# Sixteen words of padding behind a shared SBUF area, in a fused kernel of sliding-window attention and a ReLU MLP

## The chip, the cores and the metric

The kernel runs on one core of one Trainium2 chip. The metric is the device time of one execution in microseconds, taken as the median of several runs. Engines are named as the profile names them: PE (TensorE, matmuls), PEld (its weight loads), DVE (VectorE), ACT (ScalarE), POOL (GpSimd), SP (SyncE, which issues most DMAs).

## The reference

A layer over 2048 positions of width 576 adds an attention branch and an MLP branch, both on the normalized input, to the input:

```
xn  = layernorm(x)                               # x: (1, 2048, 576)
q, k, v = split(xn @ wqkv)                       # 32 heads of 18, wqkv: (576, 1728)
logits[s, w] = q[s] . k[s - 2 w] * 18 ** -0.5    # w = 0..7, masked where s - 2 w < 0
A = (softmax over w of logits, times v[s - 2 w]) @ wo      # wo: (576, 576)
B = relu(xn @ w1) @ w2                           # w1: (576, 4608), w2: (4608, 576)
out = x + A + B
```

Everything is float32 at the ends.

## The kernel before

**Phases.** The positions are dealt to two phases (even and odd), each with 1024 positions in four blocks of 256 (`NTB`, `TBN`). Within a phase the MLP's 36 hidden blocks of 128 run in two manners: six of them plainly (slots of `h_two` and `o_two`), the other thirty in 15 pairs by a seven-product scheme of Strassen's kind (`prologue`, `group`, `tail_end`). A group has eight steps; each step runs one list of products of input and W1 (`rows(...)`), and then half a piece of the second product, hidden block by W2 (`o_half`). QKV products (`qkv_half`, by four units of eight heads), attention on DVE (`attention`, fed piece by piece by `run_bg`), and the WO products (`wo_block`) are put in between. The whole order is written out by hand and by a planner that counts a matmul time of its own; the tile framework adds the waits.

**Precision.** Each float32 operand is split into a high and a low part in float32r (`two`: ACT copies the high part, DVE or POOL subtracts), and a product is a sum of three products: high by high, high by low, low by high.

**Matmuls.** Most matmuls use half of the array's rows: `mm_rows` and `rows` issue them alternately on the lower and the upper 64 partitions, so they come in pairs. In `nc.tensor.matmul(o, l, r)`, `l` is the weights operand (128 columns) and `r` is the moving operand. In the profile they stand under two lines, L140 (`mm_rows`) and L161 (`rows`); full-height ones at the start stand under L128. By tile names:

- `ph`/`pm <- xT,ar` and `xS,ar`: input (or its Strassen sums in xS) moving, 256 columns; weights are W1 or its sums, kept in `ar`.
- `po <- ar`: W2 moving, in two column parts of 256 and 320 (`CUT`); weights are the hidden blocks. Both are kept in `ar`.
- `po`/`pm <- wq,xT`: wqkv moving, 432 columns, kept in `wq` from word 60 on, with a pitch of 448 words (`WQ0`, `WQS`); weights are the input in `xT`.
- `po <- wq,att`, `wq,xS`, `att` and `att,xS`: WO moving, in parts of 256 and 320; weights are the transposed attention output.

**SBUF.** Tiles lie in a partition one after the other, in the order in which the pools are opened. In words of 4 bytes: small constants, xT (4 buffers of 2560), xS (2 of 4096 each), att (one of 68 x 144 = 9792), ar (11200), st2 (2 of 576), wq, ST (2048), and then buffers for products, evictions and small statistics. Inside `ar`: W1 and its sums from 0 on (multiples of 128 words), W2's 256-column part from 5168 (3 slots of 512), its 320-column part from 6720 (3 slots of 640), hidden blocks from 8640 (5 slots of 512):

```
W1_AT, W2A_AT, W2B_AT, H_AT, AR_WORDS = 0, 5168, 6720, 8640, 11200
```

**The area att.** The one buffer of `atp` is used by turns: for x, for q, k, v and the logits of attention (`att`), and, when attention is over, as `ot_arena`: the transposed attention output stands in 12 slots of 640 words (`ot_home`; four further slots are in xS), and behind them, from word 12 x 640 = 7680 on, stand three of the ten WO matrices of 576 columns each (`wo_rest`). The other seven stand in `wq` from its word 0 on (`wo_first`). Each WO matrix is used by `wo_half` as the moving operand, in the column parts of `CUT`.

Of the kernel before, what the change touches and what calls it, by code (L numbers as in the profile page):

```python
# [11 lines left out]
F32 = mybir.dt.float32  # L12
F32R = mybir.dt.float32r
# [6 lines left out]
P = 128  # L20
# [24 lines left out]
    (5, 0, 'xt', 6),  # L45
    (6, 0, 'xt', 7),
)
ROWS, Q_ROW, LG_ROW, K_ROW, V_ROW = 68, (15, 0), 8, 23, (38, 53)
X_AT = (2160, 2736, 0, 576, 7632, 8208, 5472, 1152)
HALO = ((0, 112), (112, 127))  # L50
# [18 lines left out]
def tile_body(ctx: ExitStack, tc: tile.TileContext, x, wqkv, wo, w1, w2, out):  # L69
    nc = tc.nc  # L70
    S, D = x.shape
    F = w1.shape[1]
    Dh = 18
    UD = HG * Dh
# [17 lines left out]
    atp = pool("atp", 1)  # L92
# [84 lines left out]
    W1, WQ, WO = {}, {}, {}  # L177
# [38 lines left out]
    def wq_load(ph, u):  # L216
        if ph == 0 and u == 0:
            z = prp.tile([P, 5, 3 * UD], F32, name="pr")
        else:
            k = V_ROW[1 if u == 0 else u % 2] * UD  # L220
            z = att(ph)[:, k : k + 15 * UD].rearrange("p (k c) -> p k c", k=5)
        WQR[ph, u] = z
        c = slice(u * UD, (u + 1) * UD)
        for kt in range(KT + 1):
            v = z[:, kt, :].rearrange("p (s c) -> p s c", s=3)
            if kt < KT:
                nc.sync.dma_start(v, wq_src[kt * P : (kt + 1) * P, :, c])
            else:
                for part in LOW, UPP:
                    nc.sync.dma_start(v[part], wq_src[KT * P : D, :, c])  # L230
# [13 lines left out]

    def wo_rest(ph):
        z = ot_arena(ph)
        WO[ph] += [z[:, 12 * 640 + k * D : 12 * 640 + (k + 1) * D] for k in range(3)]
        for kt in range(2, KT + 1):
            wo_load(ph, kt)

    def wo_load(ph, kt):
        lo = f32(WO[ph][5 + kt])
        if kt < KT:
            nc.sync.dma_start(lo, wo2[kt * P : (kt + 1) * P, :])
        else:
            for part in LOW, UPP:
                nc.sync.dma_start(lo[part], wo2[KT * P : D, :])
# [7 lines left out]
    hold = {}  # L265

    ATT = {}

    def att(ph):
        if ph not in ATT:  # L270
            ATT[ph] = atp.tile([P, ROWS * UD], F32, name="att")
        return ATT[ph]

    def ot_arena(ph):
        if ("ota", ph) not in hold:
            hold["ota", ph] = atp.tile([P, ROWS * UD], F32R, name="att")
        return hold["ota", ph]

    def load_x(i):
        z = att(0)  # L280
        k = X_AT[i]
        X[0, i] = z[:, k : k + D]
        if i < 2:
            for h, q in enumerate((nc.sync, nc.scalar)):
                c = slice(h * D2, (h + 1) * D2)
                q.dma_start(X[0, i][:, c], x_v[0, i][:, c])
            return
        nc.sync.dma_start(X[0, i], x_v[0, i])
# [28 lines left out]
    def norm(ph, i, act=False):  # L317
        nm, r = MR.pop((ph, i))
        if "xn" not in hold:
            hold["xn"] = att(0)[:, K_ROW * UD : K_ROW * UD + 1920].rearrange("p (k c) -> p k c", k=3)  # L320
        xn = hold["xn"][:, xn_count[0] % 3, 0:D]
        xn_count[0] += 1
        if act:
            nc.scalar.activation(xn, X[ph, i], AF.Identity, bias=nm)
            nc.scalar.activation(xn, xn, AF.Copy, scale=r)
        else:
            nc.vector.tensor_scalar(xn, X[ph, i], nm, r, op0=ALU.subtract, op1=ALU.mult)
            dve(600)
        XN[ph, i] = xn
# [306 lines left out]
    def ot_home(ph, i, k):  # L636
        n = 4 * WOB[ph].index(i // 2) + 2 * (i % 2) + k
        if n < 12:
            return ot_arena(ph)[:, 640 * n : 640 * (n + 1)]
        if ("otx", ph) not in hold:  # L640
            hold["otx", ph] = xsp.tile([P, 4, 640], F32R, name="xS")
        return hold["otx", ph][:, n - 12, :]
# [427 lines left out]
    def ot_plan(ph):  # L1070
        z = OTQ[ph] = []
        attended = lambda: all((ph, i) in ready for i in range(NI))
        free = lambda: attended() and ("xs", ph) in hold
        z.append(("wl", wo_rest, (ph,), attended, ()))
        for kt in range(2, KT + 1):
            z.append((("ws", kt), wo_split, (ph, kt), None, (("wl", 8 + 1.4 * (kt - 2)),)))
        for r in range(NTB):
            for i in (2 * WOB[ph][r], 2 * WOB[ph][r] + 1):
                before = 2 * WOB[ph][r - 1] + i % 2 if r else None
                z.append((("load", i), ot_load, (ph, i), attended, ((("turn", before), 0.0),) if r else ()))  # L1080
                z.append((("turn", i), ot_turn, (ph, i), None, ((("load", i), 6.0),) + (((("out", before), 4.0),) if r else ())))
                z.append((("out", i), blocks_out, (ph, i), None, ((("turn", i), 1.2),)))
                z.append((("in", i), ot_in, (ph, i), attended if r < 3 else free, ((("out", i), 5.0),)))
                z.append((("split", i), ot_split, (ph, i), None, ((("in", i), 7.0),)))
# [458 lines left out]
```

## Time and profile before

| | us |
|---|---|
| median of 3 runs | 1226.68 |
| lowest, highest of them | 1225.77, 1229.62 |
| the profiled execution, its own time | 1222.26 |
| its span, first to last instruction | 1220.5 |
| PE busy in the span | 1146.2 |
| PEld busy | 1123.8 |
| DVE busy | 813.7 |
| ACT busy | 574.9 |
| POOL busy | 473.1 |

The mean granted clock of PE in the profiled execution was 0.98. Busy times are of the span; PE and PEld overlap. A row of a group of instructions gives the line, the engine, the operation, output and inputs by tile names, the shape, the count, the busy time in us, the mean time of one in ns, and the idle time of the engine before them with what ended it. A matmul's time there holds its streaming and a fixed latency, and the latencies of consecutive matmuls overlap. A row of the timeline or of the chain gives the start in us, the length in us and what ran, with a count where equal instructions are drawn together.

### The profile page before, as it was taken

How to read it: one execution, taken by the hardware profiler on the slowest of the kernel's cores; microseconds unless marked ns; L12 is line 12 of the kernel's file. 1: busy time of each engine (PE TensorE's matmuls, PEld its weight loads, DVE VectorE, ACT ScalarE, POOL GpSimd, SP SyncE). 2: the span in 40 equal slices, each digit the busy share in tenths (PEclk: the TensorE clock that was granted, in tenths of full speed). 3: DMA queues.
4: the chain of work that ended last, by engine and by line, in shares of the span. 5: the costliest groups of instructions: out<-in, count | busy, mean ns of one | idle time of the engine just before them, and what ended most of it. 6: DMA issues, size and time to landing. Idle time of an engine off the chain costs nothing.

```text
span 1220.5 us, 38506 instructions
## 1 busy us (share of the span) xinstructions
PE 1146.2 (94%) x16410; PEld 1123.8 (92%) x16410; DVE 813.7 (67%) x1241; ACT 574.9 (47%) x1332; POOL 473.1 (39%) x522
## 2 busy tenths in 40 slices
PE   8997799999999999993899999999999999999797
PEld 8997799999999999993799999999999999999696
DVE  7564689598698687952422628876986886878331
ACT  4444564364454455552442435644644544555441
POOL 2214453353344345541221234524624533555221
PEclk9999899999999999998999999999999999999999
DMA  6467696697696588899976537857956967888996
GB/s 206 144 164 159 135 185 116 137 179 126 133 180 123 127 171 140 157 204 214 207 141 98 108 66 158 150 119 142 187 115 131 192 113 157 146 149 150 218 199 158
DMA packets 207131, 186.23 MB, mean 153 GB/s; under 512 B 69984, under 2 KB 152672, under 8 KB 206928
## 3 DMA queue, kind: packets, MB, share of 16 engines
q0 software_dynamic: 39744, 81.41, 44.9%
q1 hardware_dynamic: 166352, 101.48, 29.9%
q8 instruction: 129, 2.11, 0.7%
q10 hardware_dynamic: 864, 0.89, 0.2%
q14 instruction: 42, 0.34, 0.1%
HBM read 78.79 MB, written 100.42 MB: 147 GB/s over the span
## 4 chain that ended last, share of the span: by engine, by line
PE 72%; DMA 10%; SPq 5%; DVE 5%; issue 4%; ACT 4%; POOL 1%; ACTq 0%; DVEq 0%; POOLq 0%
PE po L161 22%; PE po L140 17%; PE ph L161 12%; PE pm L161 9%; PE pm L140 5%; PE ph L140 3%; DMA out<-ev 2%; SPq L387 2%; DMA words<-pr 2%; DVE ar L174 2%; ACT ev L703 1%; DMA att<-in_x 1%; SPq L397 1%; PE ph L128 1%; DMA xT<-words 1%
## 5 line engine op out<-in xcount | busy, mean ns | idle before, releaser
L161 PE MATMUL po<-ar 64*128 64x320 f32 (+1 forms) x5760 | 474.8, 293 | 1.5 <-DVE ar L174 0.7
L161 PEld LDWEIGHTS po<-ar 64*128 64x128 f32 x5760 | 418.1, 187 | 5.0 <-DVE ar L174 3.3
L708 POOL DMA_DIRECT2D out<-ev x276 | 244.0, 1023 | 457.1 <-ACT ev L703 429.1
L161 PE MATMUL ph<-xT,ar 64*128 64x256 f32 x2520 | 332.6, 281 | 11.7 <-ACT ar L170 6.2
L161 PEld LDWEIGHTS ph<-xT,ar 64*128 64x128 f32 x2520 | 293.7, 187 | 16.6 <-ACT pm L958 8.1
L161 PE MATMUL pm<-xS,ar 64*128 64x256 f32 x2160 | 270.4, 282 | 21.6 <-ACT u L962 15.4
L703 ACT ACTIVATE ev<-po 128x512 f32<-128x512 f32 (+1 forms) x276 | 177.7, 649 | 231.3 <-PE po L161 124.6
L161 PEld LDWEIGHTS pm<-xS,ar 64*128 64x128 f32 x2160 | 242.9, 188 | 24.1 <-ACT u L962 15.6
L174 DVE TENSOR_TENSOR ar<-st,ar 128x512 fp32r<-128x512 f32 (+3 forms) x232 | 150.4, 660 | 52.1 <-ACT ar L170 49.7
L172 POOL TENSOR_TENSOR ar<-st,ar 128x256 fp32r<-128x256 f32 (+1 forms) x72 | 94.1, 1310 | 182.5 <-ACT ar L170 180.3
L170 ACT ACTIVATE ar<-st 128x256 fp32r<-128x256 f32 (+3 forms) x304 | 148.1, 500 | 32.8 <-DMA st<-in_w 27.4
L890 POOL TENSOR_TENSOR st<-st 128x256 f32<-128x256 f32 x120 | 137.4, 1157 | 16.0 <-DMA st<-in_w 11.6
L140 PE MATMUL po<-wq,xT 64*128 64x432 f32 x1296 | 136.2, 355 | 0.0
L140 PEld LDWEIGHTS po<-wq,xT 64*128 64x128 f32 x1296 | 121.5, 184 | 3.3
L161 PE MATMUL ph<-xS,ar 64*128 64x256 f32 x720 | 107.5, 283 | 10.5 <-ACT ph L958 10.3
L161 PEld LDWEIGHTS ph<-xS,ar 64*128 64x128 f32 x720 | 97.5, 189 | 12.4 <-ACT ph L958 11.7
L560 DVE TENSOR_TENSOR pr<-att 128x1152 f32<-128x1152 f32 x64 | 87.8, 1377 | 11.3 <-DMA att<-att 11.1
L595 DVE TENSOR_TENSOR pr<-att 128x1152 f32<-128x1152 f32 x64 | 88.3, 1399 | 0.3
L563 DVE TENSOR_REDUCE att<-pr 128x64 f32<-128x1152 f32 x64 | 84.9, 1339 | 0.0
L140 PE MATMUL po<-ar 64*128 64x256 f32 (+1 forms) x984 | 75.0, 297 | 10.3 <-ACT ev L703 10.3
L140 PEld LDWEIGHTS po<-ar 64*128 64x128 f32 x984 | 68.8, 188 | 12.1 <-ACT ev L703 11.9
L602 DVE TENSOR_TENSOR pr<-pr 128x1152 f32<-128x1152 f32 x64 | 73.0, 1141 | 1.4
(117 smaller groups left out, 1313.7 us busy)
## 6 DMA issues: line engine op xcount, KB each, us to landing
out<-ev POOLq DMA_DIRECT2D x276, 288.0 KB, 5.8
st<-in_w SPq DMA_DIRECT2D x72, 288.0 KB, 4.6
st<-in_w SPq DMA_DIRECT2D x120, 128.0 KB, 4.1
att<-att SPq DMA_DIRECT2D x16, 441.0 KB, 4.5
att<-in_wqkv SPq DMA_DIRECT2D x28, 216.0 KB, 5.9
od<-att SPq DMA_DIRECT2D x32, 144.0 KB, 3.1
pr<-od SPq DMA_DIRECT2D x16, 288.0 KB, 4.9
words<-pr SPq DMA_DIRECT2D x64, 72.0 KB, 4.1
```

The costliest lines, as they stand in the source:

```text
L140: ins = nc.tensor.matmul(o, l[z], r[z], start=start, stop=stop)
L161: b.ins = nc.tensor.matmul(b.ap, l[part], r[part], start=start, stop=stop, skip_group_check=skip)
L170: nc.scalar.activation(hi, src, AF.Copy)
L172: nc.gpsimd.tensor_tensor(lo, src, f32(hi), op=ALU.subtract)
L174: nc.vector.tensor_tensor(lo, src, f32(hi), op=ALU.subtract)
L560: nc.vector.tensor_tensor(pr[i], q, window(k, i), op=ALU.mult)
L563: nc.vector.tensor_reduce(lg[:, i], pr.pop(i).rearrange(heads, d=Dh), axis=AX.X, op=ALU.add)
L595: nc.vector.tensor_tensor(pr[i].rearrange(heads, d=Dh), e, window(v, i).rearrange(heads, d=Dh), op=ALU.mult)
L602: nc.vector.tensor_tensor(o, z[:, :, 0:n], z[:, :, n : 2 * n], op=ALU.add)
L703: nc.scalar.activation(acc[:, :, cols], z[:, :, 0 : cols.stop - cols.start], AF.Copy)
L708: nc.gpsimd.dma_start(o_v[ph, 2 * tb + k], acc[:, k, :], accum_op=ALU.add)
L890: nc.gpsimd.tensor_tensor(stg(o), stg(a), stg(b), op=op)
```

## The change

The buffer of att gets 16 words more, so every tile allocated behind it (ar, st2, wq, ST and all later ones) moves up by 16 words, 64 bytes, in every partition; xT, xS and att itself stay where they are. The three WO matrices in att move up by the same 16 words within it. The view of att that attention uses keeps its size. No instruction that computes or moves data is added, removed or put elsewhere in its queue. In the built program PE, POOL and SP have the same waits as before; ACT has 14 more, each ahead of a copy of QKV results into att (L520 in `qkv_half`), for DVE's work on att in `attention`, and DVE has 6 more, each ahead of a product with v (L595 in `av_mul`), for such a copy.

```diff
+PAD = 16
 ROWS, Q_ROW, LG_ROW, K_ROW, V_ROW = 68, (15, 0), 8, 23, (38, 53)
...
     def wo_rest(ph):
         z = ot_arena(ph)
-        WO[ph] += [z[:, 12 * 640 + k * D : 12 * 640 + (k + 1) * D] for k in range(3)]
+        WO[ph] += [z[:, 12 * 640 + PAD + k * D : 12 * 640 + PAD + (k + 1) * D] for k in range(3)]
...
     def att(ph):
         if ph not in ATT:
-            ATT[ph] = atp.tile([P, ROWS * UD], F32, name="att")
+            ATT[ph] = atp.tile([P, ROWS * UD + PAD], F32, name="att")[:, 0 : ROWS * UD]
         return ATT[ph]
 
     def ot_arena(ph):
         if ("ota", ph) not in hold:
-            hold["ota", ph] = atp.tile([P, ROWS * UD], F32R, name="att")
+            hold["ota", ph] = atp.tile([P, ROWS * UD + PAD], F32R, name="att")
         return hold["ota", ph]
```

## The prediction

> **What bounds the kernel now.** I read the page first (busy shares, chain), then the stretches, then who waits for whom.
>
> ```profile
> span 1220.5 us, 38506 instructions
> PE 1146.2 (94%) x16410; PEld 1123.8 (92%) x16410; DVE 813.7 (67%) x1241; ACT 574.9 (47%) x1332; POOL 473.1 (39%) x522
> ...
> PE 72%; DMA 10%; SPq 5%; DVE 5%; issue 4%; ACT 4%; POOL 1%; ACTq 0%; DVEq 0%; POOLq 0%
> ```
>
> ```profile
> 200.00:500.00 300.00, 297.08 (x4370) 292.37 (x4369) 237.37 (x323) 150.44 (x361) 133.00 (x142) 1.00 0.75 145
> ```
>
> The columns are the stretch, its length, and the busy time of PE, PEld, DVE, ACT and POOL, then the granted clock. In this stretch PE is busy for 297.1 of 300 us, 99%, at clock 1.00, while DVE stands at 79%; the second phase has the like of it. The rest is the start, the seam between the two phases and the tail, where transfers and SP's queue enter the chain. So there is little waiting to remove: in the long stretches the time is the number of matmuls times the time of one, and a change of layout can act only on the latter.
>
> Matmuls run in pairs, one on the lower and one on the upper 64 rows, so a group of x instructions is x/2 pairs. This is what they are (mean ns of one, which is the streaming time and a latency of about 160 ns together):
>
> ```profile
> L161 PE MATMUL ph<-xT,ar 64*128 64x256 f32 x2520 | 332.6, 281 | 11.7 <-ACT ar L170 6.2 <-ACT pm L958 4.7 <-DVE ar L741 0.7
> L161 PE MATMUL pm<-xS,ar 64*128 64x256 f32 x2160 | 270.4, 282 | 21.6 <-ACT u L962 15.4 <-DVE u L967 5.5
> L161 PE MATMUL po<-ar 64*128 64x320 f32 x2880 | 261.4, 309 | 1.5 <-DVE ar L174 0.7
> L161 PE MATMUL po<-ar 64*128 64x256 f32 x2880 | 215.6, 278 | 0.0
> L140 PE MATMUL po<-wq,xT 64*128 64x432 f32 x1296 | 136.2, 355 | 0.0
> L161 PE MATMUL ph<-xS,ar 64*128 64x256 f32 x720 | 107.5, 283 | 10.5 <-ACT ph L958 10.3
> L161 PE MATMUL pm<-xT,ar 64*128 64x256 f32 x360 | 65.6, 287 | 0.1
> L140 PE MATMUL ph<-xT,ar 64*128 64x256 f32 x702 | 48.5, 286 | 3.2 <-ACT ar L170 2.3 <-DVE ar L174 0.9
> L140 PE MATMUL pm<-wq,xT 64*128 64x432 f32 x432 | 45.4, 355 | 0.0
> L140 PE MATMUL po<-ar 64*128 64x256 f32 x492 | 44.4, 283 | 8.9 <-ACT ev L703 8.9
> L140 PE MATMUL po<-wq,att 64*128 64x320 f32 x264 | 23.4, 306 | 0.0
> L140 PE MATMUL po<-wq,att 64*128 64x256 f32 x264 | 19.8, 280 | 0.0
> ```
>
> Between PE's 256-column groups lie several ns per matmul although the instruction is the same. That difference is the subject here. The time per pair comes from starts in the timeline (start, length, what):
>
> ```profile
> 621.88 1.36 PE L140 MATMUL po<-wq,att 64*128 64x256 f32 x20
> 623.08 0.40 PE L140 MATMUL po<-att 64*128 64x256 f32 x4
> ...
> 623.56 1.63 PE L140 MATMUL po<-wq,att 64*128 64x320 f32 x20
> 625.03 0.46 PE L140 MATMUL po<-att 64*128 64x320 f32 x4
> ...
> 301.40 0.88 PE L161 MATMUL ph<-xT,ar 64*128 64x256 f32 x12
> 302.12 0.86 PE L161 MATMUL po<-ar 64*128 64x256 f32 x12
> ...
> 241.97 0.86 PE L161 MATMUL po<-ar 64*128 64x256 f32 x12
> 242.67 0.87 PE L161 MATMUL ph<-xT,ar 64*128 64x256 f32 x12
> 243.37 0.86 PE L161 MATMUL po<-ar 64*128 64x256 f32 x12
> ```
>
> Ten WO pairs of 256 columns take 623.08-621.88, 120 ns each; ten of 320 take 147 ns each. So 64 more columns cost 27 ns, 0.42 ns a column. Six pairs on xT take 0.72 us in one place and 0.70 in another: 120 and 117 ns a pair. Six pairs of W2's 256-column half take 0.70 us, 117 ns, and they get faster inside the run: the group mean of a late slice of that same run (242.40 to 242.62) is 273, against 278 for the whole group:
>
> ```profile
> L161 PE MATMUL po<-ar 64*128 64x256 f32 x8 | 0.6, 273 | 0.0
> ```
>
> A WO matmul at 120 ns a pair lasts 280 ns (its group above), so 273 means 113 ns a pair: W2's half settles at 113, while WO settles at 120.
>
> **What the change does to the positions.** Count each operand's first word modulo 64 words, from the start of xT. Tiles stand in the order in which their pools are opened, and xT (4 x 2560 words), xS (2 x 4096), att (9792), ar (11200), st2 (2 x 576) are all multiples of 64, so each starts at 0. A pair streams its moving operand while the weights of the next pair are read. I call "lead" the weights' position less the moving operand's.
> - xT or xS moving at 0, weights in ar at 0: lead 0. After, ar starts at 16: lead 16.
> - W2's 256-column half, at 5168 in ar, which is 48; weights (the hidden slots at 8640) at 0: lead 16. After, both move: lead 16.
> - W2's 320-column half, at 6720, which is 0: lead 0 before and after.
> - QKV, at 60 in wq, over xT at 0: lead 4. After, 76, which is 12: lead -12.
> - WO at 0 in wq and att, over the transposed attention output at 0: lead 0. After, the padding ahead of the WO part in att keeps all WO at 16: lead -16.
>
> Before, the only class that settles at the low figure is the only one with lead 16; every class with lead 0 that runs long enough settles 7 ns above. QKV fits: its chain rows give 14 pairs in 2.74 us and 13 in 2.56, 196 to 197 ns, where 113 ns plus 176 columns at 0.42 would be 187. A matmul over the full 128 rows does the same (14 in 1.68 us, 120 ns, lead 0), so it is not the pairing.
>
> ```profile
> 12.64 1.68 PE pm L128 x14
> ...
> 283.53 2.74 PE po L140 x28
> 287.69 2.56 PE po L140 x26
> ```
>
> My reading is that two read streams of PE, moving operand and next weights, step through memory side by side and get in each other's way when they stand at the same place modulo 64 words, or nearly. The weight loads speak for it: in that full-height run at 120 one load takes 192 ns, and in the late part of the W2 run (242.30 to 242.45) 184.
>
> ```profile
> L128 PEld LDWEIGHTS pm<-xT,ar 128*128 128x128 f32 x14 | 1.8, 192 | 0.0
> L161 PEld LDWEIGHTS po<-ar 64*128 64x128 f32 x6 | 0.4, 184 | 0.0
> ```
>
> **The sum.** No instruction that computes or moves data is added, and PE's, POOL's and SP's queues keep their order and waits, so PE's time per pair can change, and 20 waits come in (point 8).
> 1. xT and xS pairs: (2520+2160+720+360+702)/2 = 3231. Now 117 to 120 ns, 118.4 taken. After, they stand as W2's half does now: between 117 (a run that follows one with another lead) and 113 (settled). I take 115, because half of these runs will follow a W2 run of the same lead and need not settle anew. 3231 x 3.4 ns = 11.0 us; ends 3231 x 1.7 = 5.5 and 3231 x 5.4 = 17.4.
> 2. W2's 256-column pairs: (2880+492)/2 = 1686. Now 117, and they will follow runs of their own lead: 114.5 taken, so 1686 x 2.2 (from 116.7) = 3.7 us; ends 0 and 1686 x 3.7 = 6.2.
> 3. QKV: 864 pairs. No row has lead -12. At best 187 for 196: 864 x 9 = 7.8 us gained; at worst another 7 ns, the price of lead 0: 6.0 us lost. Weights that trail the moving operand should be met less than weights that stand on it, so I take half of the gain, 4.0.
> 4. WO: 132 pairs of each width in the rows above, no row with lead -16: at best 7 ns each, 1.8 us; at worst as now. I take 1.2.
> 5. W2's 320-column pairs: the lead stays, nothing.
> 6. DVE, ACT, POOL: the operands of attention's products start 16 words further from one to the next (a row of q or k is 144 words), and the first two take 1.36 and 1.34 us, so a shift of 16 words costs these engines nothing that shows.
>
> ```profile
> 235.09 1.36 DVE L560 TENSOR_TENSOR pr<-att 128x1152 f32<-128x1152 f32 x1 [1.58 <-DMA att<-att]
> ...
> 238.97 1.34 DVE L560 TENSOR_TENSOR pr<-att 128x1152 f32<-128x1152 f32 x1
> ```
>
> 7. Transfers: no row shows one at two starts. I take nothing; if all of the chain's DMA share (10%, 122 us) moved by 2% either way, an estimate, that is 2.4 us. [...]
> 8. The 20 waits. A row of att is now 9808 words, no longer a whole number of 144-word rows, and the framework apparently takes the strided writes of q, k and v for wider than they are: in the built program ACT's copies of QKV into att (L520) wait 14 times for DVE's attention of the unit before, and DVE's products with v (L595) wait 6 times, three in each phase, for such copies.
>
> ```profile
> 382.77 1.19 DVE L587 TENSOR_TENSOR att<-att,r 128x512 f32<-128x512 f32 x1
> ...
> 384.22 2.82 DVE L595 TENSOR_TENSOR pr<-att 128x1152 f32<-128x1152 f32 x2
> ...
> 385.42 0.95 ACT L520 ACTIVATE att<-po 128x432 f32<-128x432 f32 x2 [3.18 <-PE po L140]
> ...
> 407.26 2.63 DVE L595 TENSOR_TENSOR pr<-att 128x1152 f32<-128x1152 f32 x2
> ...
> 408.05 0.95 ACT L520 ACTIVATE att<-po 128x432 f32<-128x432 f32 x2 [3.18 <-PE po L140]
> ...
> 416.51 0.42 DVE L967 TENSOR_TENSOR u<-u,pm 128x256 f32<-128x256 f32 x1 [3.18 <-ACT u L962]
> ```
>
> ACT's cost nothing: at 385.42 the DVE work it must wait for (382.77 + 1.19) has been over for 1.5 us, and this is the closest I found. DVE's do bite: the product that starts at 384.22 must wait for the copies that end at 385.42 + 0.95, 2.15 us later, and the one at 407.26 for 1.74 us. Six such stops, none that I found over 2.4, are 9 us of DVE as an upper end, and behind each stand the rest of attention, the low parts of hidden blocks (L741) and the sums (L967), which PE needs. What hides them: DVE sits idle for 3.18 us just before 416.51, waiting for ACT, which takes in the second stop, and PE's wait for L741 is one of 0.7 us in the whole span. Ends 0 and 9 us; I take 1.
>
> ```profile
> PE ph L161 <- DVE ar L741: 0.7, 1, 0.7
> ```
>
> The sum is 11.0+3.7+4.0+1.2 = 19.9 us of PE time. What PE gains in the long stretches comes through whole, since PE is 99% busy there; in the seam and the tail the chain runs through transfers of fixed time, and ACT and DVE, at 79% in the long stretch, will be waited for a little more often. I take 80%, 16 us, less 1 for the waits: 15. The profiled execution took 1222.3 us, 4.4 below the median of the runs, 1226.7; so 1207.3 in its terms, 1211.7 in the median's: **1212**. The case's own range: 5.5 at 80% with QKV unchanged and the waits at 1, 1223, to all best ends, 33.2 at 100%, 1194.
>
> **The rivals.**
> - *The moving operand's own start decides, whatever the weights do.* Only position 48 is good, and it belonged to W2's 256-column half alone. After the change that half stands at 0, where WO and xT now run at 120; xT and xS do not move and gain nothing: 1686 x 3.3 ns = 5.6 us slower, **1232**. It decides from the first settled W2 run. For it: the rows of before show 48 and lead 16 only together. Against: W2's matmuls come down to 273 within a run, with the moving position unchanged, and weight loads are longer where pairs take 120, which a moving stream by itself would not bring about.
> - *The same, but every second position of 16 words is good* (16 and 48, not 0 and 32). Then W2's 256 half loses 5.6 us, its 320 half (1440 pairs in L161) and WO go from 0 to 16 and gain 7 ns at most, 10.1 and 1.8: 6 us faster, **1220**. 320 columns have never been seen fast in these rows, which speaks neither way.
> - *The new waits are all that counts.* Positions do nothing, and DVE's six stops reach PE by 1 to 9 us: **1232** in the middle. It decides where a stop is longer than the time by which PE's next need of L741 or L967 lies behind; the idle 3.18 us and the lone wait of 0.7 us speak against it, DVE's 79% for it.
> - *Nothing happens.* The 113 and 120 ns would come from the length and neighbourhood of a run, not from positions: **1226.7**. Against it, W2's short runs get to 113 and the long ones of WO stay at 120. [...]
>
> **How the numbers follow.** Over 0.3% (3.7 us) is about what this kernel's runs can tell from none. Chances: my case 0.62 (0.58 of it faster, 0.04 same), the moving start alone 0.13 (slower), the waits alone 0.06 (slower), every second position 0.07 (0.05 faster, 0.02 same), nothing 0.12 (0.10 same, 0.01 to each side). That makes faster 0.64, same 0.16, slower 0.20. The range reaches from my case's low end to just past the two slower rivals: 1195 to 1234.
>
> **What would show it.** Right: by groups, xT and xS matmuls in L161 fall from 281-283 to about 277, and settled runs of them show starts 113 to 115 ns apart; W2's 256-column mean falls below 278; the 320-column mean stays at 309; weight loads stand at 184 to 185; the PE busy time falls by some 20 us with its share still near 94%. QKV's 355 tells its lead: 346 is the best end, 362 the worst. DVE shows new idle time before L595, released by ACT L520, of about 9 us. Wrong: W2's 256-column mean rises to 280 or more and xT stays (the moving start decides), the 320-column mean falls to about 300 (every second position), all means stay (nothing), or the means fall and PE's idle time behind ACT and DVE grows by as much.

## The result, and the profile after

The changed kernel took 1213.04 us in the median (1211.26 to 1215.51, 4 runs) against 1226.22 (1222.54 to 1229.62, 4 runs) for the kernel before beside it: a ratio of 0.9894, with a 95% interval of 0.9858 to 0.9931. Run again in later experiments, the same kernel took 1214.92 (1213.67 to 1222.40) against 1226.47, a ratio of 0.9918 (0.9894 to 0.9941). By these two ratios it is 10 to 13 us faster. The forecast was 1212.

The profiled execution has a span of 1209.7 us, 10.8 less than before. First the busy times, from the head of the profile page after:

```profile
span 1209.7 us, 38526 instructions
...
PE 1132.2 (94%) x16410; PEld 1110.3 (92%) x16410; DVE 810.1 (67%) x1241; ACT 573.1 (47%) x1332; POOL 474.6 (39%) x522
```

PE's busy time fell by 14.0 us with the same 16410 matmuls, that of its weight loads (PEld) by 13.5; DVE, ACT and POOL moved by less than 4. Then the groups of PE's instructions after, by form; the last two columns before the bar are busy time in us and mean ns of one. Line numbers are one higher than before (L162 was L161, L141 was L140):

```profile
L162 PE MATMUL ph<-xT,ar 64*128 64x256 f32 x2520 | 326.9, 277 | 12.6 <-ACT ar L171 6.7 <-ACT pm L959 4.9 <-DVE ar L742 0.7
L162 PE MATMUL po<-ar 64*128 64x320 f32 x2880 | 269.9, 308 | 2.7 <-DVE ar L175 2.3
L162 PE MATMUL pm<-xS,ar 64*128 64x256 f32 x2160 | 267.6, 280 | 24.7 <-ACT u L963 16.7 <-DVE u L968 7.4
L162 PE MATMUL po<-ar 64*128 64x256 f32 x2880 | 220.8, 275 | 0.0
L141 PE MATMUL po<-wq,xT 64*128 64x432 f32 x1296 | 139.9, 353 | 0.0
L162 PE MATMUL ph<-xS,ar 64*128 64x256 f32 x720 | 103.9, 277 | 5.2 <-ACT ph L959 5.0
...
L141 PE MATMUL ph<-xT,ar 64*128 64x256 f32 x702 | 46.4, 279 | 3.2 <-ACT ar L171 2.3 <-DVE ar L175 0.9
```

The xT and xS groups fell from 281 to 277, 282 to 280, 283 to 277 and 286 to 279 ns; W2's 256-column half from 278 to 275; QKV from 355 to 353; W2's 320-column half stood nearly still, 309 to 308. These means are of the whole span, with every delay and every stretch of lower clock in them, and they vary with those: the xS group at 277 ns reads 282 in a second execution of the changed kernel. In the window from 200 to 500 us, at a granted clock of 1.00, the differences are smaller and repeat. Two groups there, before and then after:

```profile
L161 PE MATMUL pm<-xS,ar 64*128 64x256 f32 x708 | 86.3, 279 | 0.0
L161 PE MATMUL po<-ar 64*128 64x256 f32 x947 | 68.9, 276 | 0.0
```

```profile
L162 PE MATMUL pm<-xS,ar 64*128 64x256 f32 x714 | 86.7, 276 | 0.2 <-DVE u L968 0.2
L162 PE MATMUL po<-ar 64*128 64x256 f32 x960 | 75.2, 274 | 0.0
```

The second execution has 276 and 274 there as well.

The prediction also expected shorter weight loads. These are the rows of one group of PEld before, after, and in a kernel with the places of after that comes below (the padding without the waits):

```profile
L161 PEld LDWEIGHTS ph<-xS,ar 64*128 64x128 f32 x720 | 97.5, 189 | 12.4 <-ACT ph L958 11.7 <-PE ph L161 0.5
```

```profile
L162 PEld LDWEIGHTS ph<-xS,ar 64*128 64x128 f32 x720 | 94.4, 185 | 7.2 <-ACT ph L959 6.4 <-PE ph L162 0.5
```

```profile
L162 PEld LDWEIGHTS ph<-xS,ar 64*128 64x128 f32 x720 | 98.2, 192 | 8.5 <-ACT ph L959 7.6 <-PE ph L162 0.5
```

189, 185 and 192 ns: a shorter weight load is not shown. The steady measure is the distance between the starts of pairs.

The clearest single place is a run of 14 pairs on xT near the start, in the timeline (start, length, what). First before, then after:

```profile
43.72 1.84 PE L140 MATMUL pm<-xT,ar 64*128 64x256 f32 x28
```

```profile
43.51 1.76 PE L141 MATMUL pm<-xT,ar 64*128 64x256 f32 x28
```

A matmul's record outlasts the distance to the next pair's start by 160 ns at 256 columns and by 159 at 320 and at 432 (medians of the undelayed pairs before); that is the latency meant here. Less about 160 ns, 14 pairs in 1.68 us are 120 ns a pair, in 1.60 us 114. Read one by one, the starts in this run lie 118, 117 and then always 120 ns apart before; after, 117, 116, 114, and then 113 to 114 to the end.

The waits of PE show that not all of this reached the end. The columns are the engine, the tile and line that waited, what it waited for, the total in us, how often, and the longest. Before:

```profile
PE pm L161 <- ACT u L962: 15.4, 1, 15.4
PE ph L161 <- ACT ph L958: 10.3, 4, 6.4
PE po L140 <- ACT ev L703: 10.3, 6, 5.0
...
PE pm L161 <- DVE u L967: 5.5, 2, 2.8
```

After:

```profile
PE pm L162 <- ACT u L963: 16.7, 1, 16.7
PE po L141 <- ACT ev L704: 15.7, 7, 6.2
PE pm L162 <- DVE u L968: 7.4, 3, 4.0
...
PE ph L162 <- ACT ph L959: 5.0, 3, 2.7
...
PE po L162 <- DVE ar L175: 2.3, 7, 0.9
```

PE waits longer for ACT's evictions (L704, where one of 4.5 us at 1163 us is new), for the sums u, and for the low parts of W2 (L175: once before, seven times now); it waits less for `ph` (L959). No single new wait carries the loss.

To see where the time went, I added up over the whole program the distances from the start of each half-height matmul to the start of the next on the same half of the array (halved, as the two halves run side by side: before, a matmul of `pm` on xS and one of `ph` on xT both start at 241.37 us, and both take 0.28 us), and sorted them. "Excess" is what undelayed pairs take above 113.3 ns for 256 columns, the lowest settled figure, and above 140 and 187 for 320 and 432, which are 113 and 0.42 ns (27 over 64) for each further column. "Delayed" pairs are those over 1.25 times these figures; their rows give what they take above them. The stretches of lower clock are 100 to 160 us, 520 to 620 us and from 1080 us on, where the granted clock is below 1 (0.91, 0.88 and, from 1100 to 1200, 0.95 before; from 1080 to 1100 it is still 1.00). The unit is us; each column is one profiled execution:

| | before | after | after, again |
|---|---|---|---|
| excess of undelayed pairs | 44.2 | 25.1 | 24.8 |
| delayed pairs, in the stretches of lower clock | 78.3 | 79.9 | 78.7 |
| delayed pairs, elsewhere | 23.0 | 30.0 | 34.1 |
| first to last matmul | 1213.9 | 1203.2 | 1205.6 |

So the pairs themselves gave 19.1 us (19.4 in the second execution), and delays took 8.5 (11.4) of it back, most of that outside the stretches of lower clock, where most of the delay is of pairs with a wait before them (19.2 of the 23.0 us before, 25.1 of the 30.0 after). (PE's busy time fell by only 14.0: of the 8.5 us of delay its idle time took 3.2, from 74.3 to 77.5 us, and the rest counts as busy, since a record of 281 ns runs on past the next start, 118.7 ns after its own.)

### The profile page after: what moved, and what is told of

The parts are those of the page before. It is cut to its first block, busy times and chain, and to the rows that moved or that the text cites. A ratio compares the mean times of both kernels' runs of the same rounds, so it can differ in the third digit from the quotient of the medians.

```text
span 1209.7 us, 38526 instructions
## 1 busy us (share of the span) xinstructions
PE 1132.2 (94%) x16410; PEld 1110.3 (92%) x16410; DVE 810.1 (67%) x1241; ACT 573.1 (47%) x1332; POOL 474.6 (39%) x522
## 5 line engine op out<-in xcount | busy, mean ns | idle before, releaser
L162 PE MATMUL po<-ar 64*128 64x320 f32 (+1 forms) x5760 | 488.8, 291 | 2.7 <-DVE ar L175 2.3
L162 PEld LDWEIGHTS po<-ar 64*128 64x128 f32 x5760 | 427.9, 185 | 6.9 <-DVE ar L175 5.4
L162 PE MATMUL ph<-xT,ar 64*128 64x256 f32 x2520 | 326.9, 277 | 12.6 <-ACT ar L171 6.7
L162 PEld LDWEIGHTS ph<-xT,ar 64*128 64x128 f32 x2520 | 290.9, 186 | 17.7 <-ACT pm L959 9.3
L162 PE MATMUL pm<-xS,ar 64*128 64x256 f32 x2160 | 267.6, 280 | 24.7 <-ACT u L963 16.7
L704 ACT ACTIVATE ev<-po 128x512 f32<-128x512 f32 (+1 forms) x276 | 177.8, 649 | 223.0 <-PE po L162 98.2
L162 PEld LDWEIGHTS pm<-xS,ar 64*128 64x128 f32 x2160 | 242.3, 187 | 27.2 <-ACT u L963 17.2
L175 DVE TENSOR_TENSOR ar<-st,ar 128x512 fp32r<-128x512 f32 (+3 forms) x232 | 148.3, 651 | 52.5 <-ACT ar L171 50.0
L141 PE MATMUL po<-wq,xT 64*128 64x432 f32 x1296 | 139.9, 353 | 0.0
L141 PEld LDWEIGHTS po<-wq,xT 64*128 64x128 f32 x1296 | 128.5, 184 | 0.0
L162 PE MATMUL ph<-xS,ar 64*128 64x256 f32 x720 | 103.9, 277 | 5.2 <-ACT ph L959 5.0
L162 PEld LDWEIGHTS ph<-xS,ar 64*128 64x128 f32 x720 | 94.4, 185 | 7.2 <-ACT ph L959 6.4
L596 DVE TENSOR_TENSOR pr<-att 128x1152 f32<-128x1152 f32 x64 | 90.2, 1429 | 8.3 <-ACT att L521 8.1
L141 PE MATMUL po<-ar 64*128 64x256 f32 (+1 forms) x984 | 74.9, 297 | 11.2 <-ACT ev L704 11.2
L141 PEld LDWEIGHTS po<-ar 64*128 64x128 f32 x984 | 68.5, 189 | 13.1 <-ACT ev L704 12.8
```

Source lines behind the costliest of these rows:

```text
L141: ins = nc.tensor.matmul(o, l[z], r[z], start=start, stop=stop)
L162: b.ins = nc.tensor.matmul(b.ap, l[part], r[part], start=start, stop=stop, skip_group_check=skip)
L175: nc.vector.tensor_tensor(lo, src, f32(hi), op=ALU.subtract)
L596: nc.vector.tensor_tensor(pr[i].rearrange(heads, d=Dh), e, window(v, i).rearrange(heads, d=Dh), op=ALU.mult)
L704: nc.scalar.activation(acc[:, :, cols], z[:, :, 0 : cols.stop - cols.start], AF.Copy)
```

## The experiments

The theory to be tested: the distance of the next weights from the moving operand, in words modulo 64, sets the time of a pair, and the waits cost next to nothing. Its rivals: the moving operand's own place decides; the absolute address, or the pools' new order, or the waits move the time.

**The padding without the waits.** A tile of 16 words of its own ahead of `ar`, and att as wide as before, so that no wait is added:

```
+    pool("padp", 1).tile([P, 16], F32, name="pad")
-            ATT[ph] = atp.tile([P, ROWS * UD + PAD], F32, name="att")[:, 0 : ROWS * UD]
+            ATT[ph] = atp.tile([P, ROWS * UD], F32, name="att")
```

> The 16 words stand in a tile of their own behind att, and WO in att moves by 16 words inside the old 9792: every operand lies where it lies in the changed kernel, and the built program has before's waits, without the 20 new ones. Lead theory: groups as in the changed kernel (xT 277, W2's 256 half 275, QKV 353), and a ratio 0 to 0.003 below the changed kernel's, since the waits were put at 1 us and at most 9. Theory that the waits eat half of the gain: 4 to 9 us (0.003 to 0.007) below it.

Measured: 1219.21 us (1211.13 to 1220.70), ratio 0.9930 (0.9907 to 0.9953); beside it, the changed kernel itself gave 0.9918 (0.9894 to 0.9941):

> The changed kernel once more, beside the three that follow. Lead theory (the two read streams of PE, the moving operand and the next weights, meet when they stand near each other modulo 64 words): ratio to before about 0.989, as measured; xT and xS matmuls at 277 to 280 ns against 281 to 283 of before. Nothing-but-noise: the ratio's interval holds 1.

The excess of the pairs is 24.3 us (after: 25.1 and 24.8), so the gain in the pairs needs only the place. The kernel is not faster than the changed one, though DVE no longer stops there (0.3 us idle before L596): the intervals overlap, and neither of the two gains expected above shows. Its profiled execution had a mean granted clock of 0.972 (after: 0.977), and its delayed pairs took 86.7 us in the stretches of lower clock (after: 79.9 and 78.7) and 32.4 elsewhere (30.0 and 34.1). Its fastest run, 1211.13, had a clock of 0.977, its slowest, 1220.70, had 0.971. This spread is larger than what the stops are worth by the next experiment.

**The waits without the padding's place.** 64 words instead of 16: the same new waits, and each place modulo 64 as before the change.

```
-PAD = 16
+PAD = 64
```

> PAD = 64: the 20 waits of the changed kernel, and every operand back at before's position modulo 64 words. Lead theory: matmul groups as before (xT 281 to 283, W2's 256 half 278, QKV 355, WO 280 and 306), ratio 1.000 to 1.002 (the waits alone, 0 to 2 us). Theory that absolute addresses matter, not those modulo 64 words: groups differ from before's. Waits-count theory: up to 9 us longer, 1.007.

Measured: 1228.47 us (1225.45 to 1231.75), ratio 1.0016 (0.9998 to 1.0034). The gain is gone, though every address behind att has moved by 64 words. From its groups of PE, and its timeline:

```profile
L162 PE MATMUL po<-ar 64*128 64x320 f32 x2880 | 261.8, 309 | 1.5 <-DVE ar L175 0.7
...
L162 PE MATMUL po<-ar 64*128 64x256 f32 x2880 | 214.9, 277 | 0.0
L141 PE MATMUL po<-wq,xT 64*128 64x432 f32 x1296 | 136.5, 355 | 0.0
L162 PE MATMUL ph<-xS,ar 64*128 64x256 f32 x720 | 107.8, 283 | 12.0 <-ACT ph L959 11.9
```

```profile
44.19 1.84 PE L141 MATMUL pm<-xT,ar 64*128 64x256 f32 x28
```

These are the figures of before: 309, 355, 283 and 1.84 us. So places count modulo 64 words (for a shift of 64 at least). The excess is 43.8 us, against 44.2. The waits are there in full, as DVE's group of the products with v shows (the last column is the idle time before it):

```profile
L596 DVE TENSOR_TENSOR pr<-att 128x1152 f32<-128x1152 f32 x64 | 89.2, 1414 | 9.4 <-ACT att L521 9.2
```

DVE stands still for 9.2 us, and the kernel is 2 us longer by the ratio, with an interval from 0 to 4.

**Which distance is good.** With the padding as a tile of its own, its size sets the distance ("lead") of xT's and xS's pairs, while W2's stays 16. One profile each:

```
-    pool("padp", 1).tile([P, 16], F32, name="pad")
+    pool("padp", 1).tile([P, N], F32, name="pad")
```

> As the kernel without the new waits, but 8 words of padding: xT and xS run at lead 8, QKV at -4, WO at -8, W2's parts as before. Lead theory with streams that meet when they stand within one 16-word piece of each other: 8 words are half a piece, so xT and xS lie between, 278 to 281 ns, nearer to lead 0; QKV about 355. If any shift away from 0 is enough: 277 to 278.

> As the kernel without the new waits, with 12 words: xT and xS at lead 12. If 16 is a narrow good place, between 8 (118.1 ns a pair) and 16 (115.1): group mean 278 to 280. If 16 is the edge of a wider one: 277.

> 20 words: xT and xS at lead 20. Narrow good place: 278 to 281, towards 32 (118.8 ns a pair). If the place widens upwards: 275 to 277, and this would be the better padding.

> 32 words: xT and xS at lead 32, QKV at -28, WO at 32. Lead theory: nothing stands near anything else, xT and xS at 277 to 280 as with 16 words, QKV 350 to 353, WO's 256 half 273 to 278. If the period were 32 words instead of 64: xT and xS back at 281 to 283 and WO's 256 half at 280.

> 48 words: xT and xS at lead 48, that is -16, weights trailing by 16; QKV at 20, WO at 16. WO in the changed kernel ran at -16 and settled at 117 to 118 ns a pair, so xT and xS are expected there too: group means 279 to 281, between lead 16 and lead 0. If leading and trailing were alike: 277.

Two of these did not test what they say: in the built programs a tile of 12 words moves `ar` by 64 bytes, 16 words, and one of 20 by 96 bytes, 24 words. The kernel called 12 thus has lead 16 (with WO's part in att at 12), the one called 20 has lead 24. The same run of 14 pairs, for tiles of 8, 12, 20, 32 and 48 words in this order:

```profile
43.88 1.82 PE L141 MATMUL pm<-xT,ar 64*128 64x256 f32 x28
```

```profile
43.25 1.76 PE L141 MATMUL pm<-xT,ar 64*128 64x256 f32 x28
```

```profile
43.71 1.80 PE L141 MATMUL pm<-xT,ar 64*128 64x256 f32 x28
```

```profile
44.30 1.82 PE L141 MATMUL pm<-xT,ar 64*128 64x256 f32 x28
```

```profile
43.62 1.83 PE L141 MATMUL pm<-xT,ar 64*128 64x256 f32 x28
```

And over the whole program: the mean distance of starts of undelayed xT pairs, and how the nearly 500 runs of at least six pairs on xT or xS end (the mean of the last two distances):

| lead of xT, xS | mean ns | quarter, median, three quarters of the runs' ends | time, us (medians for 0 and 16 (after), else one run, with before beside it) |
|---|---|---|---|
| 0 (before) | 118.7 | 119, 120, 120 | 1226.22 |
| 8 | 118.1 | 118, 118, 119 | 1225.31 (1227.63) |
| 16 (after) | 115.1 | 114, 114, 118 | 1213.04 |
| 16 (tile of 12) | 115.1 | 114, 114, 118 | 1212.84 (1226.23) |
| 24 (tile of 20) | 117.7 | 116, 117, 118 | 1223.07 (1226.23) |
| 32 | 118.8 | 116, 120, 120 | 1226.48 (1227.63) |
| 48 | 117.8 | 118, 118, 118 | 1221.78 (1227.63) |

For xT and xS the good place is narrow: only lead 16 gives runs that settle at 113 to 114 ns, and there about 70% of them end below 115.5, most others at 118; at 8, 24, 32 and 48 at most 1% do. My reading that two streams meet when they stand near each other, and part when they stand far, would have made 32 the best of all. It is as bad as 0.

But lead 16 alone does not make a pair fast. W2's 256-column pairs keep lead 16 in all of these kernels while both their places move together, and their runs of at least six pairs (about 235) end differently:

| W2's moving place, weights' place | kernel | median of the runs' ends, ns | below 115.5 |
|---|---|---|---|
| 48, 0 | before | 114 | 96% |
| 0, 16 | after | 113.5 | 70% |
| 32, 48 | tile of 48 | 113.5 | 70% |
| 8, 24 | tile of 20 | 115 | 70%, nearly all at 115 |
| 16, 32 | tile of 32 | 118 | 31% |
| 56, 8 | tile of 8 | 118 | 2% |

So the time of a pair depends on more than the distance of its two operands. Whether W2's own two places make the difference, or the xT runs that W2's runs follow and whose lead changed too, these kernels don't separate.

**W2's half at lead 0.** The same padding tile, and W2's 256-column half 16 words further, so that its moving place modulo 64 is 16 and its lead 0:

```
-W1_AT, W2A_AT, W2B_AT, H_AT, AR_WORDS = 0, 5168, 6720, 8640, 11200
+W1_AT, W2A_AT, W2B_AT, H_AT, AR_WORDS = 0, 5184, 6720, 8640, 11200
```

> As the kernel without the new waits (16 words), but W2's 256-column part moves up by 16 words inside ar, so its moving operand stands at 16 modulo 64 and its weights at 16: lead 0, while xT keeps lead 16. Lead theory: W2's 256 half goes from 276 to 278 up to 281 to 283 ns, xT and xS rise a little (279 to 281) since their runs now follow runs of another lead. Theory that every second position of the moving operand is good (16 and 48): W2's 256 half stays at 275 to 278.

```profile
L162 PE MATMUL po<-ar 64*128 64x256 f32 x2880 | 222.6, 279 | 0.0
```

```profile
43.98 1.83 PE L141 MATMUL pm<-xT,ar 64*128 64x256 f32 x28
```

1224.92 us in one run, with 1227.63 for before beside it. W2's group mean, 279 against 278 in the kernel without waits, is below the 281 to 283 expected; by starts a pair goes from 114.9 to 118.0 ns, and none of W2's runs ends below 115.5, where 73% did. A moving operand at place 16 is not good by itself, and the rival that every second position is good falls with that; nor are weights at place 16. The second fence is a surprise: the xT run, whose own lead is still 16, stays at 116 to 119 ns from start to start, although over the program 83% of the xT and xS runs end below 115.5. Lead 16 allows the 113; it does not ensure it.

**All at lead 16.** W2's 320-column half, QKV and WO moved as well:

```
-W1_AT, W2A_AT, W2B_AT, H_AT, AR_WORDS = 0, 5168, 6720, 8640, 11200
+W1_AT, W2A_AT, W2B_AT, H_AT, AR_WORDS = 0, 5168, 6704, 8640, 11200
-WQ0, WQS = 60, 448
+WQ0, WQS = 32, 448
```

> Without the new waits; besides, W2's 320-column part begins 16 words earlier, wqkv in wq 28 words earlier, and WO stands at 48 modulo 64: each class has its weights 16 words ahead of the moving operand. Lead theory: W2's 320 matmuls fall from 308 to about 300 (140 ns a pair instead of 144 to 147), QKV from 353 to 346 (187 ns a pair), WO from 284 to 273 and from 320 to 300 or so; that is 1686 x 4.5 + 864 x 5 + 216 x 4 + 216 x 6 = 14 us of PE time below the kernel without waits, of which half to 80% reaches the end: 7 to 11 us, ratio about 0.981. Theory that the moving operand's own start decides: W2's 320 part goes from 0 to 48 like W2's 256 part before, so it gains too, but xT, which stands at 0, cannot have gained in the changed kernel at all. Theory that 320 columns always take 147 ns: that group stays.

Measured: 1217.20 us (1213.66 to 1220.59), ratio 0.9922 (0.9903 to 0.9940). From its groups of PE:

```profile
L162 PE MATMUL po<-ar 64*128 64x320 f32 x2880 | 265.7, 308 | 2.4 <-DVE ar L175 1.9
...
L141 PE MATMUL po<-wq,xT 64*128 64x432 f32 x1296 | 135.8, 353 | 0.0
```

By starts, and beside the kernel with the padding tile alone, W2's 320 columns take 146.2 ns at lead 16 and 145.4 at lead 0, QKV takes 193.7 at 16 and 193.6 at -12, and xT and xS, whose lead did not change, went from 115.0 to 116.2, with 45% of their runs ending below 115.5 in place of 73%. So 320 and 432 columns don't come down to the 140 and 187 expected at 16, and moving the others changed how many of the xT runs find the low figure.

**How much of a gain on PE passes.** The positions of before, but 244 xT and xS pairs left out of the seven-product groups (one of the six products of some steps):

```
+        z[3][6] = Skip(TBN)
...
+            if all(e is not None and isinstance(e[6], Skip) for e in pair):
+                pair_time(TBN)
+                continue
```

> The kernel before, every operand at its old place, with one of six terms left out in those of Strassen's products whose two halves stand side by side: 244 pairs of 256 columns fewer, evenly over the groups of both phases; every other instruction and the order stay, and the planner counts as before. At 118.6 ns a pair 28.9 us of PE time go. Theory that PE's time goes straight to the end in the long stretches: 26 to 29 us shorter, ratio 0.977. Theory that about half of whatever PE gains is given back as waits for ACT, DVE and transfers, as in the changed kernel (22 us of pair time for 11 to 13 us): 14 to 17 us, ratio 0.987.

Measured: 1216.14 us (1212.99 to 1218.33) against 1226.23, ratio 0.9914 (0.9894 to 0.9935). 244 pairs at 118.4 ns are 28.9 us of PE time; 10.5 came through (8 to 13 by the interval), 36%, less than either expectation. In its trace the delayed pairs outside the stretches of lower clock take 39.5 us, for 23.0 before. The waits of PE in it:

```profile
PE pm L168 <- ACT u L970: 14.1, 1, 14.1
PE po L144 <- ACT ev L710: 13.9, 7, 5.4
...
PE pm L168 <- DVE u L975: 9.0, 4, 4.3
PE ph L168 <- ACT pm L966: 8.6, 17, 1.0
...
PE po L168 <- DVE ar L181: 4.6, 9, 1.5
```

These are mostly the waits that grew after the change, with another cause of PE's gain: u on DVE from 5.5 (before) to 9.0, W2's low parts from 0.7 to 4.6, the evictions `ev` from 10.3 to 13.9; `pm` on ACT, 4.7 to 8.6, comes in here. PE's share in the long stretch falls too, in the windows of this kernel:

```profile
200.00:500.00 300.00, 293.86 (x4275) 289.25 (x4274) 241.65 (x332) 151.41 (x367) 137.49 (x144) 1.00 0.78 147
```

PE fell from 297.1 us of 300 to 293.9; DVE, of whose work more falls into the same 300 us, rose from 237.4 to 241.7. That PE is 99% busy does not mean that it alone sets the time.

## Why the prediction was right, and where it was not

Time and sign came out by the mechanism forecast, a gain per pair that depends on the places of its two operands modulo 64 words. The pairs gave about what the sum had, 19.1 us for 19.9, though its terms were off both ways; less of it passed to the end than was taken; and the reading of what makes a place good was wrong.

1. *xT and xS.* 118.4 to 115 ns was taken, 118.7 to 115.1 measured: 3231 pairs by 3.6 are 11.6 us, for 11.0. Also the two ends, 113 and 117 to 118, are the two figures at which runs end.
2. *W2's 256 columns.* 116.7 to 114.5 was taken, 116.4 to 115.0 measured: 1686 by 1.4 are 2.4 us, for 3.7.
3. *QKV at lead -12.* 196.6 to 194.0, 2.6 ns by 864 are 2.2 us, for 4.0. A gain was right, but smaller than the half that was taken, and not by its reason: over the experiments QKV takes about 194 at leads of -12, -20 and 16, and 197 at 4, -4, 20 and -28, which no rule of nearness gives.
4. *WO.* In the timeline of after, ten pairs of 256 columns take 1.30 us where they took 1.36, 6 ns a pair less, and ten of 320 take 1.62 for 1.63. By all starts it is 3.0 ns for the 256 columns, 132 pairs by 3.0 or 0.4 us, for 1.2.

```profile
618.85 1.30 PE L141 MATMUL po<-wq,att 64*128 64x256 f32 x20
620.43 1.62 PE L141 MATMUL po<-wq,att 64*128 64x320 f32 x20
```

5. *W2's 320 columns* were put at nothing, since their lead stayed. They fell from 146.5 to 145.4 ns, 1686 pairs by 1.1 or 1.9 us, and stay well above 140, which is 113 and the 27 ns of 64 more columns. Why they fell at an unchanged lead isn't shown; both their places had moved, and so had the runs between which they stand.
6. and 7. *Vector engines, transfers:* nothing large shows. In the kernel without the new waits DVE's mean for L596 is 1396 ns, before it was 1399. The medians from issue to landing of the transfers that the pages list moved by 0.1 to 0.4 us, after against before: `out<-ev` from 5.8 to 6.0, `od<-att` from 3.1 to 3.5, `pr<-od` from 4.9 to 4.7.
8. *The waits.* DVE's idle time before L596 is 8.1 us, in six places, each the wait for ACT's copies that was read out of the built program; 9 was called the upper end, but six stops of up to 2.4 would be 14.4, and the kernel with 64 words has 9.2. 1 us was taken for the end; the runs give 0 to 4 (the interval of the kernel with 64 words).

```profile
DVE pr L596 <- ACT att L521: 8.1, 6, 2.0
```

Points 1 to 5 make 18.5 us, near the 19.1 by which the excess fell (44.2 to 25.1). **The step that failed is the one behind the sum: "What PE gains in the long stretches comes through whole", 80% overall.** Of 19.1 us the span kept 10.8 and the medians 11.6 and 13.2; of 19.4 in the second execution the span kept 8.1. That is 42 to 69%. In the long stretch of the first phase, matmuls 2000 to 6400, the pairs gained 5.0 us and the time 3.2; in that of the second, 9000 to 14000, 5.9 and 4.1 (in the second execution 5.1 and 2.8, 6.0 and 2.3). The window of the trace says the same in rougher form:

```profile
200.00:500.00 300.00, 295.89 (x4409) 292.09 (x4407) 238.97 (x325) 149.94 (x361) 137.18 (x144) 1.00 0.77 145
```

4409 matmuls in 300 us where there were 4370, 0.9% or 2.7 us. My reading is that the mistake was to take DVE's 79% for slack: an engine at 79% on the mean, whose results come due at fixed points of PE's order, can have points at which it is already late. That is argued, not shown: of the waits that grew the largest is on ACT (10.3 to 15.7 us), and no run makes DVE or ACT faster. The experiment with fewer products shows that part of a gain on PE is lost with another cause of the gain too. That the forecast still came within 1.1 us is in part chance. W2's 256 columns, QKV and WO gave 3.9 us less than taken, of which xT, xS and W2's 320 columns made up 2.5. And the first set of runs has the medians 13.2 us apart, for the 15 forecast, the second 11.6, which puts the changed kernel 2.9 us above the forecast.

Two signs that the prediction leaned on do not hold. Its longer and shorter weight loads (192 and 184 ns) were of different heights, 128 and 64 rows, and among loads of 64 rows the runs show no difference that repeats (189 before; 185, 190 and 192 in three executions at the new places). And W2's 256 columns, the one class that it saw settle at 113, keep their lead of 16 in kernels where they end at 118.

The rivals: that the moving start alone decides fell with W2's half (275 after, not over 280) and again with W2 at lead 0; that every second place is good fell with W2 at lead 0 and the 320 columns (308, not 300); that the weights' place alone decides, which was not among the rivals, falls too, since W2 settles at 114 with weights at 0, where xT stays at 120, and at 119 with weights at 16, where most xT runs reach 113 to 114; that the waits count alone fell with 64 words, 1.0016; that nothing happens fell with the result. The weights' place does matter to a moving operand that stays where it is: xT and xS did not move, and their pairs went from 118.7 to 115.1 ns when their weights moved by 16 words. How the one acts on the other isn't shown.

Still open: why 16 words is the good distance for xT and xS and 0, 8, 24, 32 and 48 are not; why W2's pairs at that same distance are fast at some places and slow at others; what decides whether a run settles at 113 or at 118; why 320 columns never come down to 140; and whether the kernel without the new waits is faster than the changed one, which the spread of the runs hides.

## What to carry to other kernels

Where the same matmul shows steady distances several ns apart between groups (113 and 120 here), compare the places of weights and moving operand modulo 64 words, and try a few sizes of padding, since the good one was narrow here (16 words, not 8, 24, 32 or 48) and no rule of nearness gave it. Measure it by the distances of starts, or in a window of full clock: group means of the whole span moved by as much without any change (277 and 282 ns for one group in two executions of one kernel). Before a gain on a 99% busy engine is booked as time, take a known amount of its work out and see how much arrives: here it was 36%, and of the padding's own gain 42 to 69%. And padding att, a tile that is read in strides, brought 20 waits into the built program here, and 16 words in a tile of their own brought none, so that is the cleaner way to shift what follows.

## What was not expected of the hardware

- With xT and xS at a fixed place, one place of the weights in those tried is good: 16 words ahead, most runs end at 113 to 114 ns; at 0 and 32 the median is 120, at 48 it is 118.
- The distance does not settle it: W2's runs, always at 16 words, end at 113.5 or 114 in three kernels and at 118 in two.
- With xT and xS at lead 16 there are two steady figures. About 70% of the runs end at 113 to 114 and most others at 118; in the run of 14 pairs that was read start by start, the changed kernel goes to 113 to 114 and stays, and the kernel with W2 at lead 0 stays at 116 to 119.
- A shift of 64 words gives back the figures of before (1.84 us for 14 pairs, 43.8 us of excess).
- The granted clock sinks below 1 in the same stretches in the traces of before, after and the kernel without waits, but by varying amounts (0.91, 0.89 and 0.83 at 100 to 160 us), and the time goes with it in part. Of the kernel without waits, one run took 1211.13 us at a mean clock of 0.977 and another 1220.70 at 0.971. The windows of before and of that kernel at 120 to 140 us (the third column from the end is the clock):

```profile
120.00:140.00 20.00, 13.36 (x154) 11.73 (x154) 10.29 (x21) 8.66 (x19) 8.07 (x10) 0.81 0.76 132
```

```profile
120.00:140.00 20.00, 14.16 (x146) 12.68 (x144) 9.77 (x20) 8.45 (x17) 7.29 (x9) 0.76 0.78 141
```

PE is busy for longer there, with fewer matmuls done.
